# One tile of memory results in place of two, five more row places, and a new table of slots, in a two-branch infini-attention kernel

## The chip, the cores and the metric

The kernel runs on one core of a Trainium2 chip. The metric is the time of one execution on the device in microseconds (us); lower is better. The engines are TensorE (PE; its weight loads are shown apart as PEld), VectorE (DVE), ScalarE (ACT), GpSimd (POOL) and SyncE (SP). All of the transfers that matter here are issued by SP.

## What is computed

Two attention branches A and B read the same input x (2048 tokens, 640 columns) and are mixed by a gate per token. Cut to what matters, the reference is:

```python
def branch(x, wq, wk, wv, wo, beta):             # H = 32 heads of 20, N = 4 segments of L = 512
    q, k, v = heads(x @ wq), heads(x @ wk), heads(x @ wv)
    phi = lambda t: where(t > 0, t + 1, exp(t))
    g, M, z = sigmoid(beta), 0, 0
    for s in range(N):
        p = softmax(q[s] @ k[s].T * 20**-0.5 + causal_mask)
        num, den = phi(q[s]) @ M, phi(q[s]) @ z + 1e-6
        out[s] = g * num / den + (1 - g) * (p @ v[s])
        M, z = M + phi(k[s]).T @ v[s], z + sum(phi(k[s]))
    return merge(out) @ wo
g = sigmoid((x * gate_w).sum(-1))
result = g * branch(x, A...) + (1 - g) * branch(x, B...)
```

## The kernel before

The program is a planner. While it is built, it keeps a clock and a queue for each engine, books every operation with a duration, and writes out the instructions in the order in which its own model would start them. That order is all that is left in the program: each engine runs its list from front to back and waits at semaphores. A duration in the code, such as the 0.9 in `put("D", 0.9, ...)`, is the planner's estimate; it issues nothing and delays nothing by itself.

**Passes, quads and jobs.** The work is eight passes t: segment t // 2 of branch t % 2. Each pass has eight quads of four heads, so 64 quads in all, and quad i is in pass i // 8. For a quad TensorE makes scores twice, first to find row maxima (line 1209, read by DVE in line 1196), then transposed (line 1299, read by ScalarE's exponential in line 1291 and masked by GpSimd in line 1292); then one unit multiplies the probabilities with v (line 1319, 16 calls that are recorded as 32, called the P·V unit here). Between these steps TensorE is filled with projections: a list of jobs in fixed order (`window_jobs`), each a product of one weight tile with five input tiles (line 773 in the helper `product`). For pass t it holds k tile 2, v half 0 (named 0), q and k tiles 3 and 4, v half 1 (named 4), then q and k tiles 0 and 1 of pass t + 1, the five o tiles of pass t - 1, and q tile 2 of pass t + 1. A job that can't start blocks those behind it. Products run in either half of the array, with 64 rows each, so that two run side by side.

**High and low parts.** fp32r products are made exact by splitting: each operand is a rounded high part plus a low part, and a projection adds up 15 terms: five of high by high, five with the weights' low parts, five with the input's low parts.

**Row places.** `big` is a store of NBIG places of one row tile each (128 x 512 fp32, 2 KB a partition). Nearly all that passes through SBUF takes them: input tiles (`want_x`, line 596: three places per tile, one for the load, which goes back, and one each for the high and low part, which stay until 24 jobs of the segment have read them), results of q and k on the way to DRAM, phi(q) and phi(k), attention sums, and the parts for the o projection. The planner loads segment s's input when v half 1 of the last pass of segment s - 1 begins, and asks for it with two places to spare. So at the change of a segment the old input holds 10 places until the last v product has read it, while the new one asks for 15.

**Memory results.** phi(q) times the memory (lines 883 to 900, `mem_unit`, eight units a pass) goes into a tile `O` of 10 KB a partition, five row places' worth. `O_store` has two of them: the next pass's units can write one while the results of this pass wait in the other to be transposed (`o_transpose`, line 925 by way of `turn`) and added to the attention part (line 1496). A tile goes back when its five transposes are made.

**End of a pass.** After a pass's last P·V unit the attention sums, written to DRAM by line 1364, are loaded again (1396, 1398, 1438), weighed by reciprocals (1379, 1384, 1429 or 1430), added to the transposed memory results (1496), split into parts (1420 and 1422 or 1423), and multiplied by o weights. Those weights were mixed in DRAM (571), loaded (552) and split (541, 543).

**The table.** RULES gives for quad i the order of its ten score units, by letters, and seven numbers: the share of the slot over which they are spread, how full DVE's queue may be for late units to start (`calm`), a lag between the two halves, the places that must be free for probabilities (`room`), a shift of the slot (`hold`), and two waits. A quad that is not in it keeps the values of the one ahead of it.

Of the kernel before, what the change touches and what calls it, by code (L numbers as in the profile page):

```python
# [12 lines left out]
F32 = mybir.dt.float32  # L13
# [29 lines left out]
def tile_gated_mix_infini_attn(  # L43
# [156 lines left out]
    def put(e, dur, emit, then=None, prio=5):  # L200
        heapq.heappush(ready[e], (prio, next(seq), dur, emit, then))
        load[e] += dur
        start_next(e)
# [1588 lines left out]
```

## Time and profile before

| what | value |
|---|---|
| three runs | 1014.32, 1015.88, 1016.97 us; median 1015.88 |
| profiled execution | 1016.54 us, of which the profile's span is 1014.8 |
| instructions in the span | 30,827 |
| mean granted TensorE clock | 0.995 |
| data moved by DMA | 241.99 MB, mean 238 GB/s |

The page lists for each engine the time that it was busy in the span, and a chain of waits that ends with the last instruction. A matmul in one half of the array counts TensorE as busy, even when the other half has nothing. In the tables by stretch the columns are the stretch, its length, the busy time of PE, PEld, DVE, ACT and POOL with the number of instructions, the granted clock, the share of DMA time and GB/s. In a timeline a row is start, duration, engine, line, operation, output <- inputs and count, with the idle time ahead of it and what ended that in brackets. Groups by line show the count, busy time in all, and the mean of one in ns.

### The profile page before, as it was taken

To read this page: it belongs to the slowest core of one execution; us is meant where nothing else is said; L and a number is where in the kernel's file an instruction comes from. 1 tells how busy PE (TensorE), PEld (TensorE's weight loads), DVE (VectorE), ACT (ScalarE), POOL (GpSimd) and SP (SyncE) were. 2 spreads that over 40 slices of the span, in tenths; PEclk is the share of its full clock that TensorE was granted. 3 is DMA by queue.
4 is the path that set the end of the run, shared out by engine and by line. 5 is a ranking of instruction groups with operands and counts; after the bars stand their busy time and mean duration, and the time that the engine had idled before them with its cause. 6 is when DMAs were issued, how large, how long until landed. Compare 5 with 4: busy or idle time off the path is not lost.

```text
span 1014.8 us, 30827 instructions
## 1 busy us (share of the span) xinstructions
PE 1002.1 (99%) x11260; PEld 855.5 (84%) x11260; DVE 769.3 (76%) x2604; ACT 659.5 (65%) x1341; POOL 612.3 (60%) x1040
## 2 busy tenths in 40 slices
PE   9999999999999999999999999999999999999998
PEld 7998888888888888878888878897889888878876
DVE  4688777976787778877578976888567897689764
ACT  5376776776566767757766666675676666675672
POOL 4465657676476655775646656486675656567571
PEclk9999999999999999999999999998999999999999
DMA  7999989898896988866768687795876979688531
GB/s 248 308 306 270 298 255 305 274 283 259 262 286 185 286 237 245 268 183 219 237 177 300 188 267 234 206 301 175 252 230 182 313 213 281 206 228 267 151 93 62
DMA packets 148886, 241.99 MB, mean 238 GB/s; under 512 B 13216, under 2 KB 46144, under 8 KB 148416
## 3 DMA queue, kind: packets, MB, share of 16 engines
q1 hardware_dynamic: 148736, 240.03, 77.2%
q8 instruction: 89, 1.46, 0.6%
q14 instruction: 61, 0.50, 0.2%
HBM read 150.83 MB, written 94.65 MB: 242 GB/s over the span
## 4 chain that ended last, share of the span: by engine, by line
PE 84%; DMA 6%; DVE 5%; ACT 1%; POOL 1%; issue 1%; SPq 1%; ACTq 0%; DVEq 0%; POOLq 0%
PE bank L773 50%; PE bank L1319 13%; PE bank L1299 7%; PE bank L1209 7%; PE bank L883 3%; PE bank L965 3%; PE bank L925 2%; DMA row<-dots 1%; DMA dots<-row 1%; DMA kd<-row 1%; DVE bank L1196 1%; PE bank L1234 1%; DVE row L1429 1%; DVE row L1422 1%; DMA row<-in_xT_dram 1%
## 5 line engine op out<-in xcount | busy, mean ns | idle before, releaser
L1196 DVE CUSTOM_DVE_ANT_0 bank<-bank,tri 128x256 f32<-128x256 f32 (+3 forms) x1024 | 474.7, 520 | 150.2 <-PE bank L1209 96.8
L773 PE MATMUL bank<-row,wh 64*128 64x512 f32 x2308 | 498.6, 403 | 0.6 <-DVE mw L897 0.6
L1291 ACT ACTIVATE p<-bank 128x512 f32<-128x512 f32 x588 | 324.0, 601 | 140.0 <-PE bank L1299 108.4
L1292 POOL TENSOR_SCALAR_AFFINE_SELECT p<-p 128x256 f32<-128x256 f32 (+1 forms) x588 | 219.2, 380 | 228.6 <-ACT p L1291 219.2
L773 PEld LDWEIGHTS bank<-row,wh 64*128 64x128 f32 x2308 | 319.8, 186 | 11.8 <-issue 1.1
L773 PE MATMUL bank<-row,wl 64*128 64x512 f32 x1154 | 293.3, 402 | 0.0
L543 POOL TENSOR_TENSOR wl<-wst,wh 128x640 fp32r<-128x640 f32 x115 | 181.3, 1581 | 58.1 <-ACT wh L541 51.7
L1209 PE MATMUL bank<-kst,qst 60*128 60x384 f32 (+3 forms) x1024 | 184.0, 317 | 1.8 <-DVE row L1349 0.8
L773 PEld LDWEIGHTS bank<-row,wl 64*128 64x128 f32 x1154 | 173.6, 186 | 5.0 <-issue 0.6
L1299 PE MATMUL bank<-qst,kst 62*128 62x128 f32 (+3 forms) x1024 | 176.4, 317 | 1.0 <-ACT vst L1015 0.5
L773 PE MATMUL bank<-wvh,row 64*128 64x320 f32 x1280 | 176.7, 312 | 0.0
L1319 PE MATMUL bank<-p,vst 128*32 128x384 f32 (+3 forms) x1936 | 148.9, 431 | 0.0
L773 PEld LDWEIGHTS bank<-wvh,row 64*128 64x128 f32 x1280 | 147.4, 185 | 1.0 <-issue 0.2
L1196 DVE DVE_READ_ACCUMULATOR2_ANT mx<- 128x1 f32 x1024 | 144.6, 141 | 0.0
L1209 PEld LDWEIGHTS bank<-kst,qst 60*128 60x128 f32 x1024 | 137.5, 186 | 8.2 <-DVE row L1349 1.2
L1299 PEld LDWEIGHTS bank<-qst,kst 62*128 62x128 f32 x1024 | 130.5, 186 | 7.3 <-DVE mx L1196 1.0
L1319 PEld LDWEIGHTS bank<-p,vst 128*32 128x32 f32 x1936 | 59.3, 110 | 87.4 <-issue 62.7
L541 ACT CAST wh<-wst 128x640 fp32r<-128x640 f32 x119 | 86.4, 741 | 20.2 <-PE bank L773 14.4
L773 PE MATMUL bank<-wvl,row 64*128 64x320 f32 x640 | 99.3, 310 | 0.0
L1349 ACT COPY row<-bank 128x512 f32<-128x512 f32 x61 | 36.0, 590 | 79.4 <-PE bank L1319 71.1
L773 PEld LDWEIGHTS bank<-wvl,row 64*128 64x128 f32 x640 | 80.0, 185 | 0.6 <-issue 0.4
L518 POOL TENSOR_TENSOR wvl<-wst,wvh 128x640 fp32r<-128x640 f32 (+1 forms) x48 | 64.0, 1338 | 17.3 <-ACT wvh L515 17.3
(117 smaller groups left out, 1213.5 us busy)
## 6 DMA issues: line engine op xcount, KB each, us to landing
qst<-qd SPq DMA_DIRECT2D x128, 240.0 KB
kst<-kd SPq DMA_DIRECT2D x128, 240.0 KB
qd<-row SPq DMA_DIRECT2D x40, 512.0 KB
kd<-row SPq DMA_DIRECT2D x40, 512.0 KB
dots<-row SPq DMA_DIRECT2D x56, 256.0 KB
wst<-wmix SPq DMA_DIRECT2D x35, 320.0 KB
row<-dots SPq DMA_DIRECT2D x42, 256.0 KB
qd<-row SPq DMA_DIRECT2D x40, 256.0 KB
```

Of the source, the lines that this page charges most:

```text
L518: put("G", 0.77 * n, lambda: nc.gpsimd.tensor_tensor(out=wl[:, a:b, :], in0=w3, in1=r32(wh[:, a:b, :]), op=ALU.subtract), end, prio=4)
L541: put("A", 0.625, lambda: nc.scalar.copy(wh, w3), lambda: put(lo_eng, lo_cost, lambda: lo.tensor_tensor(out=wl, in0=w3, in1=r32(wh), op=AL ...
L543: lambda: lo.tensor_tensor(out=wl, in0=w3, in1=r32(wh), op=ALU.subtract), end, prio=3), prio=6)
L773: return nc.tensor.matmul(bank_of, lhsT=w[ROWS[half]], rhs=x_[ROWS[half]], start=start, stop=stop)
L883: return nc.tensor.matmul(pm[:, a - h0:c - h0, :].rearrange("p h e -> p (h e)"), lhsT=r32(pqTs[t, m][ROWS[half], P * n:P * (n + 1)]), rhs= ...
L1196: put("D", w / 960.0 + 0.105, lambda: nc.vector.tensor_tensor_reduce(out=sc[:, off:off + w], in0=sc[:, off:off + w], in1=tri[:, L - w:], s ...
L1209: lane_ops[half].append((mm(w), lambda pair=pair, qb=qb, off=off, w=w, r=r, sc=sc: nc.tensor.matmul(sc[:, off:off + w], lhsT=q[r, pair, P ...
L1291: put("A", 0.483, lambda: nc.scalar.activation(pt, sc, AF.Exp, scale=SCALE), lambda: (bank.give(sc), put("G", 0.15 + 0.105 * len(todo), la ...
L1292: "G", 0.15 + 0.105 * len(todo), lambda: nc.gpsimd.affine_select(out=blocks, in_=blocks, pattern=[[0, len(todo)], [1, P]], base=0, channel ...
L1299: lane_ops[half].append((mm(w), lambda pair=pair, kb=kb, off=off, w=w, r=r, sc=sc: nc.tensor.matmul(sc[:, off:off + w], lhsT=k[r, pair, P ...
L1319: nc.tensor.matmul(po[32 * j:32 * j + 32, P * kb:], lhsT=vst[t % 2][:, kb, h * E1:h * E1 + 32], rhs=pts[i, n, f][0][:, off:off + w], start ...
L1349: either(0.483, lambda: nc.scalar.copy(r32(oT), po), 0.605, lambda: nc.vector.tensor_copy(r32(oT), po), end, 2)
```

## The change

Four things change: `O_store` holds one tile, `NBIG` goes from 29 to 34 (the same memory), six estimates of row operations go up, and every line of the table is new.

```diff
-        4: "TSTSTSTSTS 1.010 1.52 0.31 8 1.9 1.31 1.66",
+        4: "STTSTSSTST 1.010 1.53 0.26 4 0.0 0.35 1",
...
-    NBIG, NWST, NWH, SPARE = 29, 3, 4, 2
+    NBIG, NWST, NWH, SPARE = 34, 3, 4, 2
...
-    O_store = Store([sb.tile([P, NB, D], F32, tag=f"O{i}", name=f"O{i}", bufs=1) for i in range(2)])
+    O_store = Store([sb.tile([P, NB, D], F32, tag=f"O{i}", name=f"O{i}", bufs=1) for i in range(1)])
...
-            put("D", 0.9, lambda: nc.vector.scalar_tensor_tensor(
+            put("D", 1.0, lambda: nc.vector.scalar_tensor_tensor(
                 out=r32(d), in0=r32(d), scalar=gcol[t % 2], in1=r32(g), op0=ALU.mult, op1=ALU.mult), lambda: half(0), prio=2)
...
-                D=(0.85, lambda: nc.vector.tensor_tensor(out=lo, in0=r32(y), in1=r32(hi), op=ALU.subtract)),
-                G=(1.25, lambda: nc.gpsimd.tensor_tensor(out=lo, in0=r32(y), in1=r32(hi), op=ALU.subtract))), prio=2)
+                D=(0.95, lambda: nc.vector.tensor_tensor(out=lo, in0=r32(y), in1=r32(hi), op=ALU.subtract)),
+                G=(1.35, lambda: nc.gpsimd.tensor_tensor(out=lo, in0=r32(y), in1=r32(hi), op=ALU.subtract))), prio=2)
...
-                D=(0.9, lambda: nc.vector.tensor_tensor(out=r32(y), in0=r32(y), in1=r32(r), op=ALU.mult)),
-                G=(1.4, lambda: nc.gpsimd.tensor_tensor(out=r32(y), in0=r32(y), in1=r32(r), op=ALU.mult)))
+                D=(1.05, lambda: nc.vector.tensor_tensor(out=r32(y), in0=r32(y), in1=r32(r), op=ALU.mult)),
+                G=(1.5, lambda: nc.gpsimd.tensor_tensor(out=r32(y), in0=r32(y), in1=r32(r), op=ALU.mult)))
```

The table has one line more in the changed kernel, so line numbers behind it are higher by one there: line 773 of before is line 774.

What this does to the order shows at three places. The first is the change to segment 2 of the input, in pass 3, on two engines. On SP, `dots_119` holds the sums of pass 2, and `dots_120` those of pass 3. Before, the last rows ahead of and with the fifth input load are:

```order
L1364 DMA dots_120<-row_8348_6985 128x512
L1438 DMA row_8370_7010<-dots_119 128x1x512
L1246 DMA qst_82<-mr_163 2x8x128 x2
L552 DMA wst_144<-wmix_130 128x5x128
L1438 DMA row_8448_7075<-dots_119 128x1x512
L1438 DMA row_8466_7090<-dots_119 128x1x512
L1438 DMA row_8487_7106<-dots_119 128x1x512
L1167 DMA qst_81<-qd_100 60x2x512 x2
L596 DMA row_8566_7159<-in_xT_dram 128x512
L1167 DMA kst_85<-kd_108 60x2x512 x2
```

The other four loads stand 13 to 19 rows ahead of that one. In the changed kernel the five stand within nine rows, around the write of the last sums of pass 2:

```order
L597 DMA row_7878_6566<-in_xT_dram 128x512
L1168 DMA qst_83<-qd_100 60x2x512 x2
L1365 DMA dots_119<-row_7966_6631 128x512
L1168 DMA kst_87<-kd_108 60x2x512 x2
L1247 DMA qst_81<-mr_161 2x8x128 x2
L597 DMA row_7883_6569<-in_xT_dram 128x512
L597 DMA row_7946_6611<-in_xT_dram 128x512
L597 DMA row_7963_6630<-in_xT_dram 128x512
L597 DMA row_8006_6666<-in_xT_dram 128x512
L553 DMA wst_142<-in_a_wq_dram 128x640
```

The fifth load has moved from behind the reloads of pass 2's sums to ahead of all of them.

On TensorE at the same change, before, ahead of the first product on the new columns (`row_8112` with `wh`), these rows end a run without any projection; `O` is the tile of memory results, `mbd` the memory, `mt` the row maxima:

```order
L925 MATMUL bank_141<-ident,O_158 128x64 x4
L883 MATMUL bank_135<-mbd_2_77,row_7211_6017 128x21
L883 MATMUL bank_138<-mbd_4_79,row_8327_6960 128x84
L883 MATMUL bank_135<-mbd_3_78,row_7932_6631 128x84
L883 MATMUL bank_135<-mbd_4_79,row_8327_6960 128x84
L1234 MATMUL bank_136<-ident,mt_7269 32x64
L1299 MATMUL bank_139<-qst_82,kst_86 128x512
L1299 MATMUL bank_137<-qst_82,kst_86 128x512
L883 MATMUL bank_135<-mbd_3_78,row_7932_6631 128x84
L1234 MATMUL bank_136<-ident,mt_7269 32x64
L883 MATMUL bank_135<-mbd_4_79,row_8327_6960 128x84
L773 MATMUL bank_141<-row_8112_6774,wh_145 128x512
```

In the changed kernel the products on the new columns (`row_7877` to `row_8004`) alternate with the v products (`wvl`) on the old ones (`row_29..`):

```order
L774 MATMUL bank_135<-row_7944_6609,wl_148 128x512
L1210 MATMUL bank_137<-kst_87,qst_83 128x128
L774 MATMUL bank_138<-wvl,row_2916_2591 128x320
L774 MATMUL bank_135<-row_7961_6628,wl_148 128x512
L774 MATMUL bank_138<-wvl,row_2921_2594 128x320
L774 MATMUL bank_135<-row_8004_6664,wl_148 128x512
L774 MATMUL bank_138<-wvl,row_2926_2597 128x320
L774 MATMUL bank_138<-wvl,row_2931_2600 128x320
L774 MATMUL bank_135<-row_7877_6565,wh_147 128x512
L1300 MATMUL bank_140<-qst_81,kst_85 128x384
```

The run without projections between the two inputs is gone from this place: the q product on the new columns has begun 59 matmuls ahead of the last v product on the old ones, where it stood 82 behind.

The second place is SP's list in pass 1, where the mixed o weights of branch A are made ready for the o jobs of pass 0. Before:

```order
L571 DMA wmix_130<-wrow_128 32x2560
L1364 DMA dots_118<-row_3704_3181 128x512
L571 DMA wmix_130<-wrow_128 32x2560
L1246 DMA qst_83<-mr_163 2x8x128 x2
L752 DMA kd_107<-row_3811_3250 128x2x512
L752 DMA kd_107<-row_3812_3251 128x512
L552 DMA wst_144<-wmix_130 128x5x128
L552 DMA wst_143<-wmix_130 128x5x128
L552 DMA wst_142<-wmix_130 128x5x128
```

And now:

```order
L1168 DMA kst_84<-kd_106 60x2x512 x2
L640 DMA wst_143<-in_x_dram 128x640
L572 DMA wmix_130<-wrow_128 32x2560 x2
L753 DMA kd_107<-row_3583_3110 128x2x512
L753 DMA kd_107<-row_3584_3111 128x512
L553 DMA wst_144<-wmix_130 128x5x128
L553 DMA wst_142<-wmix_130 128x5x128
L553 DMA wst_143<-wmix_130 128x5x128
```

`kd_107` is the DRAM copy of pass 2's k; the write shown is that of its tile 0 in both. The last two mixes now follow each other, a row ahead of that write, and the second write of sums (`dots_118`, of pass 1) no longer stands between them.

The third place is the memory matmuls (line 883) on TensorE. The 44 of a pass stood in two groups, some 50 us of TensorE's work apart; in passes 3 to 7 they now stand together, behind the transposes of the pass before, and in passes 4 and 6 with hardly a projection among them. From pass 4, in the changed kernel:

```order
L774 MATMUL bank_134<-row_8005_6665,wh_145 128x512
L774 MATMUL bank_135<-row_8005_6665,wh_151 128x512
L884 MATMUL bank_141<-mbd_0_70,row_8633_7207 128x84
L884 MATMUL bank_137<-mbd_0_70,row_8633_7207 128x84
L884 MATMUL bank_141<-mbd_1_71,row_8938_7521 128x84
L884 MATMUL bank_137<-mbd_1_71,row_8938_7521 128x84
L884 MATMUL bank_141<-mbd_2_72,row_9624_8093 128x63
```

Eleven more rows of memory matmuls and a P·V unit follow before the rest of them.

119 rows, old and new, of the table RULES are left out of this document.

## The prediction

> **What bounds the kernel now.** I read the page first, then the stretches in which TensorE's projections pause, then the queue that feeds them. The page gives busy time by engine and the chain that ended last.
>
> ```profile
> span 1014.8 us, 30827 instructions
> PE 1002.1 (99%) x11260; PEld 855.5 (84%) x11260; DVE 769.3 (76%) x2604; ACT 659.5 (65%) x1341; POOL 612.3 (60%) x1040
> PE 84%; DMA 6%; DVE 5%; ACT 1%; POOL 1%; issue 1%; SPq 1%; ACTq 0%; DVEq 0%; POOLq 0%
> ```
>
> TensorE is the bound, with 84% of the chain. The 99% hides waits, since a small matmul in one half of the array counts as busy while the other half is empty. So I looked for places where TensorE runs no projection at all. Two stand out, both where segment 2 or 3 of the input begins. In the timeline of TensorE (start, duration, instruction) the last product on the old columns is the v product, line 773 with wvl; the next projection is the first q product on the new ones.
>
> ```profile
> 427.58 0.30 PE L773 MATMUL bank<-wvl,row 64*128 64x320 f32 x1
> 437.87 1.26 PE L773 MATMUL bank<-row,wh 64*128 64x512 f32 x4
> 684.97 0.39 PE L773 MATMUL bank<-wvl,row 64*128 64x320 f32 x1
> 696.20 0.47 PE L773 MATMUL bank<-row,wh 64*128 64x512 f32 x1
> ```
>
> That is 10.3 us and 11.2 us without a projection. What they wait for is the fifth input tile: SP issues its load only once the old columns have been given back, and ScalarE's cast (L586) sits idle until it lands.
>
> ```profile
> 411.00 1.53 SPq L596 DMA_DIRECT2D row<-in_xT_dram  x3
> 428.27 0.40 SPq L596 DMA_DIRECT2D row<-in_xT_dram  x1
> 435.91 0.62 ACT L586 CAST row<-row 128x512 fp32r<-128x512 f32 x1 [2.16 <-DMA row<-in_xT_dram]
> 685.38 1.45 SPq L596 DMA_DIRECT2D row<-in_xT_dram  x1
> 691.55 0.62 ACT L586 CAST row<-row 128x512 fp32r<-128x512 f32 x1 [2.73 <-DMA row<-in_xT_dram]
> ```
>
> Four of five loads are out by 412.5; the fifth leaves at 428.27, within 1 us of the last v product, and lands 7.6 us later. So what is missing is row places, which is what the change adds. The stretches themselves (PE busy, weight loads, DVE, ACT, POOL, granted clock, DMA share, GB/s):
>
> ```profile
> 427.60:437.90 10.30, 8.65 (x122) 6.70 (x119) 10.10 (x28) 6.37 (x14) 8.78 (x10) 1.00 0.91 287
> 437.90:442.00 4.10, 4.10 (x22) 3.22 (x23) 2.77 (x9) 2.17 (x5) 4.10 (x6) 0.58 0.27 73
> 685.00:696.20 11.20, 10.41 (x105) 6.70 (x104) 9.22 (x25) 4.78 (x11) 8.35 (x8) 0.70 0.79 242
> ```
>
> TensorE is truly idle for 1.65 and 0.79 us. The granted clock falls to 0.58 over the 4.1 us behind the first stretch (1.7 us lost) and to 0.70 inside the second (3.4 us lost). The same P·V unit shows it:
>
> ```profile
> 430.74 2.36 PE L1319 MATMUL bank<-p,vst 128*32 128x512 f32 x32
> 691.33 3.86 PE L1319 MATMUL bank<-p,vst 128*32 128x512 f32 x32
> 436.98 0.23 PE L1234 MATMUL bank<-ident,mt 64*32 64x64 f32 x1 [1.59 <-POOL mt L1221]
> ```
>
> **The change, part by part.** The counts of instructions on TensorE are the same before and after; only the order moves.
>
> *Input waits (gain).* The order puts all five loads of segments 2 and 3 ahead of the load of the sums, and the first new product 59 and 48 matmuls ahead of the last v product, where it stood 82 and 69 behind. Does the data come in time?
>
> ```profile
> 400.58 1.16 PE L1319 MATMUL bank<-p,vst 128*32 128x384 f32 x20
> 426.50 0.40 PE L773 MATMUL bank<-row,wh 64*128 64x512 f32 x1
> 426.74 0.40 PE L773 MATMUL bank<-row,wh 64*128 64x512 f32 x1
> 402.91 0.58 SPq L1364 DMA_DIRECT2D dots<-row  x1
> 417.77 0.62 ACT L586 CAST row<-row 128x512 fp32r<-128x512 f32 x1 [0.68 <-DMA qst<-qd]
> L590 POOL TENSOR_TENSOR row<-row,row 128x512 fp32r<-128x512 f32 x15 | 19.6, 1320 | 2.2 <-ACT row L586 2.2
> ```
>
> Between the P·V unit of quad 23 and that product the order now has 43 products of 512 columns, 100 of 320, 36 scores, 20 transposes and one P·V unit. A 512-column product of one half takes 0.24 us, from the two starts, so 0.12 us with both halves in use, and the shorter ones (scores have 320 on the mean) in proportion; with the P·V unit, 2.3, that is 18 us. "Us of work" is counted in this way from here on.
>
> The write of quad 23's sums goes out 1.2 us after its P·V unit ended (401.7); two small writes and four loads later it is about 5 us. From the last of the three loads (412.1) to the last cast's end was 6.3 us, so high parts by about 12 us and, at 1.3 us each on GpSimd (L590), low parts by 17, which the product needs only at its eleventh term. It fits, with some 3 us to spare; quad 39 has 17 us and fits likewise.
>
> What is saved? The work inside the stretches is not removed but goes beside projections: in the first, one P·V unit, 42 transposes, 19 memory matmuls (two passes each) and 4 scores; in the second one P·V unit, 36, 14 and 2.
>
> ```profile
> 433.72 0.47 PE L925 MATMUL bank<-ident,O 64*128 64x64 f32 x8
> 434.74 0.65 PE L883 MATMUL bank<-mbd,row 64*128 64x84 f32 x6
> ```
>
> Eight transposes take 0.47 us of which 0.22 is one's own length, so 0.036 apart; memory passes (0.65 - 0.27)/5 = 0.076. First stretch: 2.3 + 42 x 0.036 + 38 x 0.076 + 4 x 0.12 = 7.2 of 10.3 us, saved 3.1. Second: 2.3 + 1.3 + 2.1 + 0.2 = 5.9 of 11.2, saved 5.3 with its own half-rate clock in it. With 1.7 for the clock behind the first: **10.0 us**. The lower bound is idle time and clock alone, 2.4 + 5.1 = 7.5. The upper: beside projections the small matmuls take one of two halves and cost half, which saves 5.5 + 7.1 + 1.7 = 14.3. I take the middle, as the rows just read are the nearest.
>
> Rows for the clock's part stand above: 1.59 us of idle, and the lower clock follows directly. [...]
>
> *One tile of memory results (cost).* The memory matmuls of a pass now wait until the pass before has handed back the tile. In passes 4 and 6 all 44 stand within 6 us of work, in 3, 5 and 7 within 19; before they were split over some 50. Each of eight units needs three operations on DVE:
>
> ```profile
> L897 DVE SCALAR_TENSOR_TENSOR mw<-bank,gq 128x19 f32<-128x19 f32 (+1 forms) x48 | 8.1, 168 | 9.4 <-PE bank L883 9.4
> L899 DVE RECIPROCAL mw<-mw 128x19 f32<-128x19 f32 (+1 forms) x48 | 12.4, 258 | 1.6
> L900 DVE TENSOR_TENSOR O<-bank,mw 128x380 f32<-128x380 f32 (+1 forms) x48 | 23.6, 491 | 1.6
> ```
>
> That is 0.92 us, 7.3 for eight, and the banks stay taken meanwhile. Their cover is the q and k jobs of the next pass. In passes 4 and 6 DVE needs 1.3 us more than TensorE has work; I take **1.0 us** in all, with 0 (the next products cover it) and 12.5 (the second rival) as ends.
>
> *The o jobs of pass 0 (cost).* They now begin 37 us of work after that pass's last P·V unit, before 49. Their weights come by a chain that the trace shows whole:
>
> ```profile
> 188.60 0.86 SPq L571 DMA_DIRECT2D wmix<-wrow  x1
> 194.87 1.84 SPq L552 DMA_DIRECT2D wst<-wmix  x3
> 202.06 1.36 ACT L541 CAST wh<-wst 128x640 fp32r<-128x640 f32 x2
> 202.87 3.08 POOL L543 TENSOR_TENSOR wl<-wst,wh 128x640 fp32r<-128x640 f32 x2 [0.23 <-ACT wh L541]
> L965 PE MATMUL bank<-vst,row 64*128 64x147 f32 (+1 forms) x480 | 64.3, 293 | 0.0
> L733 ACT ACTIVATE row<-row 128x512 f32<-128x512 f32 x25 | 16.1, 656 | 0.1
> ```
>
> From the last mix to the first low part (202.87 + 1.54) it is 15.8 us. In the new order that mix stands just ahead of the write of k tile 0, whose product ends 14 us of work before the first o product (60 products, 18 scores, 26 transposes, one P·V unit, and 22 updates of two passes at half of 64.3/480 us); with 2 us for taking that product out of its bank the mix may go 12 to 16 us ahead. So TensorE waits 0 to 4 us; I take **0.5**, as SP has few rows there to be held by.
>
> *The rest.* The planner's raised costs (0.9 to 1.0 and so on) issue nothing; they and the table act by the order alone. Nine more phi tiles take the way with a second activation (L733): 9 x 0.656 = 5.9 us more on ScalarE, hidden since it is 65% busy, and 5.9 if it bound. Behind the last P·V unit 8.4 us of work stand, before 9.65; the end is a chain of transposes and DVE, so I count nothing (0 to +1).
>
> The sum: -10.0 + 1.0 + 0.5 = -8.5 us. The profiled execution took 1016.54 (span 1014.8 and 1.7 around it), 0.66 above the median of 1015.88, so 1008.0 for it and **1007.4** against the median.
>
> **Rivals.** One more row, of the low part that ended pass 2's chain:
>
> ```profile
> 441.11 1.29 POOL L1423 TENSOR_TENSOR row<-row,row 128x512 fp32r<-128x512 f32 x1
> ```
>
> - *The wait moves on to the o jobs* (1013.5). The o products of pass 2 come 42 us of work after quad 23's P·V unit, before 47; in the trace the last low part came 40.7 us after it (442.4). For: four input loads and two weights now stand ahead of the sums. Against: the five loads of rows are no longer held for places. Three us late at passes 2 and 4, and the weights' ends above, give back 6.
> - *The bunched memory units hold TensorE* (slower, 1020). At five boundaries DVE takes 7.3 us of memory units in one go, and the row maxima (L1196) queue behind; in the first stretch DVE was busy for 10.10 of 10.30 us. If TensorE stands for 2.5 us at each, 12.5 us are added. It makes the change a loss from 2 us at each on. Against: the planner starts no such unit while DVE's queue is long.
> - *The small matmuls cost half* (1002): the upper bound of the gain with both costs at nothing.
> - That places still lack is excluded by the order, unless the loads themselves come late.
>
> **How the numbers follow.** A measurement here tells about 0.3%, 3 us, from no change: faster is below 1012.8, slower above 1018.9. Forecast 0.60 (by itself 1002 to 1012), the wait that moves 0.20, bunching 0.13, half cost 0.07. All of the forecast and the half cost, and 0.08 of the moved wait, are faster: 0.75. The rest of the moved wait, 0.12, is the same; bunching, 0.13, slower. The range 1000 to 1017 leaves out bunching and about 0.05 below.
>
> **What would show it.** The five input loads of segments 2 and 3 stand together on SP, none after the last v product; no stretch of 10 us without line 773 at these places; a granted clock of 1.00 at both; PE's share of the chain up, DMA's down. Wrong: a new stretch without projections before the first o product of pass 0, 2 or 4, or DVE near 100% with TensorE waiting on line 897 or 1196 after the transposes of O.

## The result, and the profile after

The changed kernel takes **1017.18 us** (median of 18 runs, 1014.32 to 1019.94), the kernel before 1014.27 in the same comparison (18 runs, 1012.20 to 1016.97). The ratio is 1.0026, with a 95% interval of 1.0017 to 1.0035: 2.9 us slower, where 1007.4 had been forecast.

Nearly every sign that the prediction named for its main step came true all the same. The page of the changed kernel, busy times and chain:

```profile
span 1016.0 us, 30827 instructions
...
PE 1004.5 (99%) x11260; PEld 859.7 (85%) x11260; DVE 766.3 (75%) x2593; ACT 663.9 (65%) x1352; POOL 612.5 (60%) x1040
...
PE 89%; DMA 4%; DVE 4%; ACT 1%; issue 1%; SPq 0%; POOL 0%; DVEq 0%; POOLq 0%; ACTq 0%
```

TensorE's share of the chain rose from 84 to 89%, DMA's fell from 6 to 4%, and the mean granted clock is 0.999. On SP the loads of segments 2 and 3 stand together:

```profile
405.79 1.86 SPq L597 DMA_DIRECT2D row<-in_xT_dram  x4
...
660.87 3.40 SPq L597 DMA_DIRECT2D row<-in_xT_dram  x5
```

The stretches around the two segment changes (the same columns as in the prediction) show TensorE idle for 0.39 us of the first 22, for none of the others, and a granted clock of 1.00:

```profile
413.00:435.00 22.00, 21.61 (x245) 18.94 (x242) 16.38 (x45) 14.47 (x30) 15.53 (x21) 1.00 0.95 291
...
670.00:692.00 22.00, 22.00 (x242) 19.93 (x240) 19.80 (x48) 16.25 (x34) 17.72 (x21) 1.00 0.88 288
692.00:711.00 19.00, 19.00 (x242) 16.98 (x238) 17.38 (x49) 12.89 (x26) 11.68 (x18) 1.00 0.93 309
```

So what the prediction took for a wait is gone, and the kernel is slower. To see where the time went I counted TensorE's work at the prediction's prices (0.12 us for a product of 512 columns and in proportion for shorter ones and scores, 2.3 for a P·V unit, 0.036 for a transpose, 0.076 for a memory pass, 0.067 for an update pass; 977.4 us in both kernels) and took it from the time between P·V units. What is left over is loss: waits, an empty half, a low clock. Here it is by pass, each from the end of the last P·V unit of the pass before to the end of its own:

| loss in us, profiled execution | pass 0 | 1 | 2 | 3 | 4 | 5 | 6 | 7 | behind | sum |
|---|---|---|---|---|---|---|---|---|---|---|
| before | 7.6 | 2.0 | 1.9 | **6.5** | 1.9 | **5.3** | 0.3 | 6.4 | 5.6 | 37.4 |
| changed | 7.6 | 4.4 | 3.3 | 3.4 | 1.8 | 1.6 | 2.9 | 7.4 | 6.2 | 38.6 |

The passes with a change of input (3 and 5) lose 6.8 us less, about what TensorE's idle time and the low clock took in that execution of before (7.5 by the prediction), and not 10. Passes 1, 2, 6 and 7 lose 7.4 us more. The prices are estimates. If the small matmuls are counted by their columns alone, passes 3 and 5 gain 5.9 us, pass 1 loses 1.5 and pass 6 again 2.6, but pass 2 then gains 1.6 and pass 7 loses 3.7, so of these two the table says little. (By these two executions the changed kernel is 1.2 us behind, by the medians 2.9: the one of before took 1016.54, 2.3 above its median.)

One more view decides how this is to be read. Each execution comes with its mean granted clock. Over the 90 executions of before in all comparisons with the experiments the mean is 0.9966 (0.993 to 0.998); the one that the prediction was made from had 0.995. Over 18 executions of the changed kernel it is 0.9995. The difference, 0.0029 of 1014, is 2.9 us of clock gained, if TensorE is what counts throughout. So, by this estimate, everything else got worse by 2.9 + 2.9 = 5.8 us. (Among the executions with six added matmuls, below, 0.0063 of clock goes with 4.2 us of time; by that rate it would be 1.9 and 4.8.)

### The profile page after: what moved, and what is told of

The parts are those of the page before. It is cut to its first block, busy times and chain, and to the rows that moved or that the text cites. A ratio compares the mean times of both kernels' runs of the same rounds, so it can differ in the third digit from the quotient of the medians.

```text
span 1016.0 us, 30827 instructions
## 1 busy us (share of the span) xinstructions
PE 1004.5 (99%) x11260; PEld 859.7 (85%) x11260; DVE 766.3 (75%) x2593; ACT 663.9 (65%) x1352; POOL 612.5 (60%) x1040
## 4 chain that ended last, share of the span: by engine, by line
PE 89%; DMA 4%; DVE 4%; ACT 1%; issue 1%; SPq 0%; POOL 0%; DVEq 0%; POOLq 0%; ACTq 0%
PE bank L774 52%; PE bank L1320 14%; PE bank L1300 7%; PE bank L1210 7%; PE bank L966 3%; PE bank L884 3%; PE bank L926 2%; DMA kd<-row 1%; DVE bank L1197 1%; PE bank L1235 1%; DMA row<-dots 1%; DMA qd<-row 1%; DVE row L1430 1%; DMA row<-rowg 1%; DMA wst<-in_a_wk_dram 1%
## 5 line engine op out<-in xcount | busy, mean ns | idle before, releaser
L1197 DVE CUSTOM_DVE_ANT_0 bank<-bank,tri 128x384 f32<-128x384 f32 (+3 forms) x1024 | 473.9, 520 | 155.2 <-PE bank L1210 121.5
L774 PE MATMUL bank<-row,wh 64*128 64x512 f32 x2308 | 507.2, 403 | 1.2 <-DVE mx L1197 0.7
L1292 ACT ACTIVATE p<-bank 128x512 f32<-128x512 f32 x568 | 312.4, 599 | 138.4 <-PE bank L1300 108.4
L774 PEld LDWEIGHTS bank<-row,wh 64*128 64x128 f32 x2308 | 323.8, 185 | 12.5 <-issue 1.3
L774 PE MATMUL bank<-row,wl 64*128 64x512 f32 x1154 | 298.0, 399 | 0.0
L774 PE MATMUL bank<-wvh,row 64*128 64x320 f32 x1280 | 181.3, 312 | 0.0
L1300 PE MATMUL bank<-qst,kst 62*128 62x512 f32 (+3 forms) x1024 | 178.2, 318 | 1.9 <-DVE mw L898 0.7
L1320 PE MATMUL bank<-p,vst 128*32 128x512 f32 (+3 forms) x1896 | 142.1, 424 | 0.0
L1210 PEld LDWEIGHTS bank<-kst,qst 60*128 60x128 f32 x1024 | 132.4, 186 | 8.9 <-DVE mx L1197 4.0
L774 PE MATMUL bank<-wvl,row 64*128 64x320 f32 x640 | 104.5, 310 | 0.0
```

The costliest lines, as they stand in the source:

```text
L774: return nc.tensor.matmul(bank_of, lhsT=w[ROWS[half]], rhs=x_[ROWS[half]], start=start, stop=stop)
L1197: put("D", w / 960.0 + 0.105, lambda: nc.vector.tensor_tensor_reduce(out=sc[:, off:off + w], in0=sc[:, off:off + w], in1=tri[:, L - w:], s ...
L1210: lane_ops[half].append((mm(w), lambda pair=pair, qb=qb, off=off, w=w, r=r, sc=sc: nc.tensor.matmul(sc[:, off:off + w], lhsT=q[r, pair, P ...
L1292: put("A", 0.483, lambda: nc.scalar.activation(pt, sc, AF.Exp, scale=SCALE), lambda: (bank.give(sc), put("G", 0.15 + 0.105 * len(todo), la ...
L1300: lane_ops[half].append((mm(w), lambda pair=pair, kb=kb, off=off, w=w, r=r, sc=sc: nc.tensor.matmul(sc[:, off:off + w], lhsT=k[r, pair, P ...
L1320: nc.tensor.matmul(po[32 * j:32 * j + 32, P * kb:], lhsT=vst[t % 2][:, kb, h * E1:h * E1 + 32], rhs=pts[i, n, f][0][:, off:off + w], start ...
```

## The experiments

Three theories stood against each other at first. A: the places save what was forecast and the new table gives it away. B: one tile of memory results costs about what the places bring. C: a table fits only the order that it was found with. In all that follow "before" is the kernel before, run on the same chip in the same rounds.

### What the table does

The first two exchange the tables between the kernels; the last two give both the same single line for all slots:

```diff
     RULES = {
-        0: "STTSTSSTST 1.010 1.71 0.30 8 0.0 1.73 1",
...
+        0: "TSTSTSTSTS 1.010 2.38 0.30 8 0.0 1.6 1",
     }
```

> The changed kernel with the table of slots of before; one tile of memory results, 34 places and the raised estimates stay. Theory A (the places save what was forecast, some 7 to 9 us, and the new table gives it away by shifting small waits): 1006 to 1010. Theory B (one tile of memory results costs about as much as the five places bring, whatever the table): 1014 to 1020. Theory C (each table fits only the order that it was found with, and any other loses some us): 1018 to 1026, above the changed kernel's 1017.2.

> The kernel before with the new table only. Theory A (the new table gives away what the places bring): 1020 to 1024, since the 7 to 9 us that the table costs are then without the places' gain. Theory B (the table does nothing by itself): 1012 to 1017. Theory C (a table fits only its own order): 1018 to 1026.

> The kernel before with one line for all 64 slots, the values that most lines of both tables have, so that no slot is set by hand. Only the difference from the next run counts for the stores; its height over 1014.3 is what the table of before is worth: A and B 1014 to 1020, C 1020 or more.

> The changed kernel with the same single line for all slots. Against the run before it, Theory A (places save, the new table loses): 7 to 9 us faster. Theory B (one tile costs what the places bring): within 3 us, or slower. Theory C says nothing of the sign, but both stand some 5 us or more above 1014.3.

| kernel | median, us | ratio to before (95%) | planner's own end, us |
|---|---|---|---|
| before | 1015.25 | 1 | 1005.4 |
| changed | 1017.18 | 1.0026 (1.0017 to 1.0035) | 1005.9 |
| changed, table of before | 1064.58 | 1.0479 (1.0456 to 1.0501) | 1048.5 |
| before, new table | 1068.87 | 1.0521 (1.0494 to 1.0548) | 1050.5 |
| before, one line | 1059.68 | 1.0431 (1.0407 to 1.0456) | 1043.5 |
| changed, one line | 1059.22 | 1.0451 (1.0416 to 1.0485) | 1048.6 |

The planner's own end is the clock that the program keeps while it is built; it is no measured time. All four missed what A and B expected, and the exchanged tables cost much more than C had allowed: each table is worth some 45 us to the stores and estimates that it was found with. The wrong table is 9 us worse than one line in before, and in the changed kernel no better than one line. With one line for all slots the stores make no difference that shows: 1059.68 and 1059.22 us, uncertain by some 4. Two things follow. A change of four parts can't be taken apart by undoing one, since each part alone makes a new plan without its table. And the planner had reckoned with the missing places all along, since it books them itself: by its own clock the two plans end 0.5 us apart.

So the remaining experiments leave the order alone. They change what an instruction does, not when the planner books it, and each engine's list stays the same but for what the edit names.

### Is the stretch a wait?

The fifth input tile of segments 2 and 3 is not loaded; its cast reads a tile that is there:

```diff
-                put("A", 0.515, lambda: nc.scalar.copy(hi, r32(st)), low, prio=6)
+                put("A", 0.515, lambda: nc.scalar.copy(hi, r32(src)), low, prio=6)
...
-            dma(0.87, lambda: nc.sync.dma_start(
+            dma(0.87, lambda: None if skip else nc.sync.dma_start(
```

> The kernel before with its order of instructions unchanged, but the fifth input tile of segments 2 and 3 is left out: its two loads are not issued, and its casts read the first tile's high part, which is there. So the result is computed from a wrong fifth tile; what is measured is the time without the transfer's 7.6 us. Theory W (the two stretches cost the 2.4 us of idle and the 5.1 of lower clock, and their other work costs the same wherever it stands): 1007 to 1010. Theory F (the forecast's fuller gain, 10 or more): 1004 or less. Theory N (the wait is made up for behind it): 1013 or more.

> The same omission in the changed kernel, whose fifth loads stand with the other four: a control. If the five more places have taken the input waits away, nothing is left to gain: 1016 to 1018. If the loads still hold TensorE there, 1010 to 1014. As in the run before it, the fifth tile of segments 2 and 3 is wrong.

Before without the fifth loads: 1014.61 us, ratio 1.0000 (0.9988 to 1.0012). The changed kernel: 1016.51, ratio 1.0020 (1.0010 to 1.0031). Theory N was right for before: **the transfer of the fifth tile costs nothing there.** The timeline of before without it shows why. The cast no longer waits, but TensorE still runs 8.6 us of other work between its last v product and the next q product:

```profile
426.83 0.30 PE L778 MATMUL bank<-wvl,row 64*128 64x320 f32 x1
435.46 0.97 PE L778 MATMUL bank<-row,wh 64*128 64x512 f32 x4
...
432.90 0.62 ACT L591 CAST row<-row 128x512 fp32r<-128x512 f32 x1
```

Its stretches (the columns as before) show the first one full at a clock of 1.00, and the second as before, with the clock at 0.70 on the mean, though there is nothing to load:

```profile
426.80:435.50 8.70, 8.62 (x123) 6.76 (x119) 8.64 (x22) 6.54 (x14) 8.70 (x11) 1.00 0.92 288
...
682.10:693.60 11.50, 10.43 (x106) 6.75 (x106) 9.33 (x25) 4.82 (x11) 8.35 (x8) 0.70 0.68 214
```

And the idle time of the first stretch differs between executions. Here it is in the seventh run (e7), which keeps the order and the fifth load of before and leaves out some work of DVE: the load lands 6.0 us after its issue instead of 7.6, ScalarE waits 0.45 us for it instead of 2.16, and the stretch (its row stands behind the two of the timeline) is full at a clock of 1.00:

```profile
426.51 0.40 SPq L596 DMA_DIRECT2D row<-in_xT_dram  x1
...
432.47 0.62 ACT L586 CAST row<-row 128x512 fp32r<-128x512 f32 x1 [0.45 <-DMA row<-in_xT_dram]
```

```profile
425.90:434.50 8.60, 8.52 (x120) 6.66 (x117) 8.57 (x22) 6.34 (x14) 8.60 (x10) 1.00 0.88 289
```

From P·V unit 24 to 26 the profiled execution of before took 40.4 us; with the same instructions there, two other profiled executions took 37.2 (e10, where TensorE idles for 0.08 us in the stretch) and 38.5 (e9, 0.81 us, with the clock at half for 3.4 us behind it). So the wait is real in some executions and absent in others.

### Do the bunched memory units hold TensorE?

Two of a memory unit's three operations on DVE are left out:

```diff
-            nc.vector.scalar_tensor_tensor(
-                out=w, in0=pm[:, :nh, DH], scalar=1e-6, in1=gq[t][:, n, h0:h1], op0=ALU.add, op1=ALU.mult)
-            nc.vector.reciprocal(w, w)
+            w = gq[t][:, n, h0:h1]
```

> The kernel before, order unchanged, without two of the three DVE operations of each memory unit (the weights with the normaliser, 168 ns, and their reciprocal, 258 ns): the memory result is multiplied by the gates alone, so it is not normalised. 96 operations and about 20 us of DVE fewer. Theory B (memory units in one go on DVE hold TensorE): within 2 us of 1014.3, since they are spread here. If DVE's lateness at every boundary counts, whatever the units' spread: 1009 to 1012.

> The same omission in the changed kernel, where the eight units of a pass stand together. Theory B (bunched units hold TensorE, 2 to 3.5 us at some of five boundaries): 3 to 6 us faster than the changed kernel, 1011 to 1014, and clearly more than the run before it gains. Theory R (what the change loses is many small shifts of the order, not these units): the same gain as in the run before it, 0 to 2 us.

Before: 1013.31 us, ratio 0.9984 (0.9973 to 0.9996). Changed: 1016.25, ratio 1.0019 (1.0008 to 1.0030). The first gains 0.16%, 1.6 us; the second, from 1.0026, 0.07%, 0.7 us. If the bunched units held TensorE, the changed kernel would gain more, not less. Theory B is out, and with it the mechanism of the prediction's slower rival. The pair also shows that some 20 us less work on DVE does not by itself bring the two kernels together.

### What is the clock worth, and what lets it fall?

Six and twelve matmuls were added where TensorE stands in the second stretch, all into unused columns of a memory unit's bank:

```diff
+    FILL = {('mem', 161): 1, ('mem', 164): 1, ('S', 703): 1, ('mem', 167): 3}
...
+        for _ in range(FILL.get((kind, seen[kind]), 0)):
+            nc.tensor.matmul(last[:, 400:], lhsT=ident, rhs=ident[:, :112], start=True, stop=True, skip_group_check=True)
```

> The kernel before with six more matmuls (128 rows, 112 columns, into unused columns of the memory unit's bank) in the second stretch, where TensorE stands for 0.3 and 0.35 to 0.65 us and the granted clock then falls to 0.50 for 3.3 to 6.8 us. Theory K (what the change gained is the lower clock of this stretch, and TensorE's standing there lets it fall): the clock stays up, the mean clock of the runs goes from 0.9967 to 0.999, and the time from 1014.6 to 1011.5 to 1012.5. If the small matmuls themselves pull the clock down: the six cost up to 1 us and the clock is as before, 1014.5 to 1015.5.

> The same with twelve. Theory K: the clock stays up, but the twelve need some 2 us and the standing covers 1: 1012.5 to 1013.5. Otherwise 1015 to 1016.5.

With six, 1015.82 us, ratio 1.0009 (0.9994 to 1.0024); with twelve, 1014.90, ratio 1.0001 (0.9984 to 1.0018). The medians say nothing; the clocks do. No execution of before, of 90, had a mean clock above 0.998. With six added matmuls 6 of 12 had 1.000 (mean span 1011.9 us), and 4 had 0.993 or 0.994 (1016.1). With twelve, 9 of 11 had 1.000. The stretch in the profiled execution of each, six first, then twelve:

```profile
682.00:694.00 12.00, 11.83 (x89) 9.38 (x89) 10.61 (x35) 6.07 (x12) 8.86 (x10) 0.70 0.89 283
```

```profile
682.00:694.00 12.00, 11.88 (x140) 9.15 (x139) 10.39 (x29) 5.68 (x12) 8.91 (x10) 1.00 0.83 250
```

So twelve added matmuls keep the clock up in nine executions of eleven, and six in half of them. That TensorE's standing is what lets it fall, as the prediction took it, is not shown. In the execution with six, TensorE stood for 0.17 us in these 12 us, and the clock was at half for 10.2 us. In before the clock fell at 687.6, ahead of the second standing. And without DVE's multiplications (e11, below) TensorE stood for 0.81 us at the same place, and the clock stayed up:

```profile
683.00:691.00 8.00, 7.19 (x105) 5.00 (x104) 6.77 (x21) 4.61 (x11) 7.14 (x8) 1.00 0.92 290
```

The twelve matmuls (two records each) took 3.7 us themselves, in the timeline of their own execution:

```profile
684.01 0.70 PE L871 MATMUL bank<-ident 128*128 128x112 f32 x4
685.37 0.70 PE L871 MATMUL bank<-ident 128*128 128x112 f32 x4
686.82 0.92 PE L871 MATMUL bank<-ident 128*128 128x112 f32 x6
688.10 1.37 PE L871 MATMUL bank<-ident 128*128 128x112 f32 x10
```

That is about what they saved: from P·V unit 40 to 42 it is 42.2 us with and without them (45.5 in the execution with six). Theory K was right that the clock can be held up there and wrong on the profit; what lets it fall stays open.

The clock was at half for 6.8 us in before (687.6 to 694.4), for 3.4 in e7 (685.2 to 688.6) and for 10.2 in e9 (686.8 to 697.0). In e7 TensorE had stood for 0.32 and 0.65 us ahead of that. What sets these lengths was not shown either.

### DVE's row operations

TensorE's first standing in that stretch (0.31 us) was for DVE, the second (0.35 us) for ScalarE. In before a multiplication of two rows took 1.92 us while GpSimd worked on a weights' low part, and the addition behind it, which gives back the bank, came late:

```profile
684.98 1.54 POOL L543 TENSOR_TENSOR wl<-wst,wh 128x640 fp32r<-128x640 f32 x1 [0.17 <-ACT wh L541]
...
685.14 1.92 DVE L1429 TENSOR_TENSOR row<-row,row 128x512 f32<-128x512 f32 x1
686.99 0.68 DVE L1496 TENSOR_TENSOR row<-bank,row 128x512 f32<-128x512 f32 x1
...
687.72 0.80 PE L1209 MATMUL bank<-kst,qst 60*128 60x512 f32 x2 [0.31 <-DVE row L1496]
```

Is that common? The groups of such operations show it, here the low parts of before; the line of 0.69 us is the same kind of operation early in the kernel:

```profile
L1422 DVE TENSOR_TENSOR row<-row,row 128x512 fp32r<-128x512 f32 x16 | 18.2, 1148 | 0.0
...
L590 DVE TENSOR_TENSOR row<-row,row 128x512 fp32r<-128x512 f32 x5 | 3.4, 692 | 2.0 <-ACT row L586 1.9
```

Sorted by whether GpSimd ran a two-operand operation during more than a tenth of them, the 40 operations of before take 0.74 us on the mean (10, none beside) and 1.24 (30, up to 1.92), those of the changed kernel 0.76 (10) and 1.31 (30, up to 1.93). It is not only operations of two operands: the one-operand copies of the runs below take 0.42 us alone, and 1.01 (e13) and 1.07 (e14) on the mean beside GpSimd's. The traces show that the long ones go with GpSimd's work, not how it slows them. In all, the 40 operations take 44.7 us in before and 46.9 in the changed kernel.

Theory D: these operations, with the row maxima queued behind them, are what the changed order loses by. Two pairs of runs leave them out, first the multiplications alone, then all that stand at the end of a pass:

```diff
-                D=(0.9, lambda: nc.vector.tensor_tensor(out=r32(y), in0=r32(y), in1=r32(r), op=ALU.mult)),
+                D=(0.9, lambda: None),
```

```diff
-            put("D", 0.9, lambda: nc.vector.scalar_tensor_tensor(
-                out=r32(d), in0=r32(d), scalar=gcol[t % 2], in1=r32(g), op0=ALU.mult, op1=ALU.mult), lambda: half(0), prio=2)
+            put("D", 0.9, lambda: None, lambda: half(0), prio=2)
...
-                D=(0.85, lambda: nc.vector.tensor_tensor(out=lo, in0=r32(y), in1=r32(hi), op=ALU.subtract)),
+                D=(0.85, lambda: nc.vector.tensor_copy(lo, r32(hi))),
```

> The kernel before, order unchanged, without the 12 multiplications by reciprocals that stand on DVE (line 1429; 0.96 to 1.92 us each, the long ones while GpSimd works on rows too), so these rows of the attention part stay unweighed. Theory D (DVE's row operations at the end of a pass hold the row maxima, and so TensorE): 1.5 to 3 us faster, mostly in the second stretch, whose first standing is behind the one of 1.92 us. If they are hidden: within 1 us of 1014.6.

> The same omission in the changed kernel, which has 14 of them on DVE. Theory D (what the changed order loses at quads 9, 40, 49 and 58 stands behind these operations): 3 to 5 us faster than 1017.2, more than the run before it gains. If the loss has other causes: at most as much as the run before it gains.

> The kernel before, order unchanged, without DVE's row operations of two operands in SBUF at the end of a pass: the 12 multiplications by reciprocals and the 7 gatings are left out, and the 16 low parts are copies of the high part (one operand). 41 us of DVE less some 10 for the copies. Theory D (these hold row maxima and so TensorE): 1007 to 1010, little below the run that left out the multiplications alone (1009.9), since before has its stall behind one of those. Theory O (the order itself): no less than that run.

> The same omission in the changed kernel (14 multiplications, 7 gatings, 14 low parts on DVE). Theory D: the difference between the two kernels goes away, 1007 to 1010, and the steps at quads 49 and 58, which stand behind a gating of 1.93 and a low part of 1.80 us, are gone. Theory O: the changed kernel stays 2 to 3 us above the run before it, 1010.5 to 1013, and the steps stay.

| left out on DVE | before, us | ratio to before (95%) | changed, us | ratio to before (95%) |
|---|---|---|---|---|
| nothing | 1014.27 | 1 | 1017.18 | 1.0026 (1.0017 to 1.0035) |
| multiplications | 1009.87 | 0.9954 (0.9939 to 0.9970) | 1012.89 | 0.9983 (0.9968 to 0.9997) |
| all three kinds | 1011.31 | 0.9960 (0.9943 to 0.9976) | 1010.12 | 0.9948 (0.9934 to 0.9963) |

The multiplications alone (0.69 to 1.92 us each in before, where the expectation says 0.96 to 1.92) gain 0.46% in before (4.7 us) and 0.43% in the changed kernel (4.4), more than was expected of before and no more in the changed one: on this pair Theory D failed. In before they also end the second stretch's stall: 39.1 us from P·V unit 40 to 42 instead of 42.2, with the clock at 1.00 where it had been at half for 6.8 us. With gatings and low parts gone too, the changed kernel gains 0.78% (7.9 us) and before 0.40% (4.1; 1011.3 where Theory D had expected 1010 at most), and the changed one is no longer the slower: by the two ratios it stands at 0.9988 of the other, uncertain by 0.0022. **The difference of +0.26% has become -0.12%**, a shift of 0.38% with 0.24% of uncertainty (the three half widths of the intervals, 0.09, 0.165 and 0.145, as the root of their squares): 3.9 us of the 5.8, uncertain by 2.4. By the middle value Theory O is out for the larger part of the loss. The copies that replace the low parts still take 14.9 and 13.6 us, so what was left out is 26 us of DVE in before and 30 in the changed kernel.

The waits for DVE's row maxima (`mx`) say more than the times. A score can't take its bank before the row maximum of an earlier one has been read out of it. These are the weight loads of scores that stood for that (us in all, how often, the longest), before first, then changed, then changed without the row operations (e14):

```profile
PEld bank L1299 <- DVE mx L1196: 1.0, 3, 0.5
PEld bank L1209 <- DVE mx L1196: 0.4, 2, 0.2
```

```profile
PEld bank L1210 <- DVE mx L1197: 4.0, 9, 0.9
PEld bank L1300 <- DVE mx L1197: 2.5, 6, 0.8
```

```profile
PEld bank L1210 <- DVE mx L1197: 0.5, 2, 0.3
PEld bank L1300 <- DVE mx L1197: 0.2, 1, 0.2
```

The sums are alike in all profiled executions of the two orders: 1.4 to 2.0 us in the seven of the order of before that keep some or all of these operations, 4.2 to 6.5 in the five such of the changed order, and 0.2 and 0.7 with all three kinds left out. Without the multiplications alone it is still 4.3 in the changed order (e12), which fits that pair's result. Weight loads waited while earlier matmuls still ran: in the changed kernel the matmuls of these two lines stood for 1.2 and 0.7 us where their weight loads stood for 4.0 and 2.5, so not all of this is TensorE's time.

A place that shows it is behind P·V unit 48, in pass 6. In the changed kernel a gating takes 1.93 us beside GpSimd's low part, the row maximum queued behind it comes late, and the two scores that need its bank wait:

```profile
796.25 1.56 POOL L544 TENSOR_TENSOR wl<-wst,wh 128x640 fp32r<-128x640 f32 x1
...
796.43 1.93 DVE L1380 SCALAR_TENSOR_TENSOR row<-row,gcol,row 128x512 f32<-128x512 f32 x1 [0.96 <-DMA row<-dots]
798.28 0.69 DVE L1197 CUSTOM_DVE_ANT_0 bank<-bank,tri 128x512 f32<-128x512 f32 x1
...
798.10 0.33 PE L1210 MATMUL bank<-kst,qst 60*128 60x384 f32 x1
799.08 0.44 PE L1210 MATMUL bank<-kst,qst 60*128 60x384 f32 x2 [0.65 <-DVE mx L1197]
```

Without the row operations (e14) the same scores follow the same fifteen v products at once:

```profile
791.63 1.33 PE L774 MATMUL bank<-wvh,row 64*128 64x320 f32 x15
792.77 0.42 PE L1210 MATMUL bank<-kst,qst 60*128 60x384 f32 x4
```

Times between P·V units of the changed order, which can be compared directly since the lists are the same: from 48 to 49 it is 24.2, 23.1 and 23.0 us in the changed kernel, e6 and e8, and 22.2 in e14; from 39 to 40 it is 16.0, 15.5 and 16.4, and 15.2; from 57 to 58 it is 16.7, 16.7 and 16.8, and 16.4. The gating of 1.93 us took 0.78 in e6 and 0.79 in e8, so of the 2.0 us between 24.2 and 22.2 half belongs to one execution. By the count of loss by pass, the changed order loses 2.6 us more than that of before in pass 6, and 0.5 more without the row operations (e14 against e13). In pass 1 it is 2.4 and 3.3: that loss has another cause, which stays open.

The last two runs move the multiplications instead of leaving them out, a candidate for a version better than both:

```diff
-                D=(0.9, lambda: nc.vector.tensor_tensor(out=r32(y), in0=r32(y), in1=r32(r), op=ALU.mult)),
+                D=(0.9, lambda: nc.gpsimd.tensor_tensor(out=r32(y), in0=r32(y), in1=r32(r), op=ALU.mult)),
```

> The kernel before with the 12 multiplications issued to GpSimd at the same place of the order, all of the result computed. Theory D: DVE's row maxima come earlier, 1010 to 1013, if GpSimd (60% busy) can take 12 x 1.3 us where they stand. If GpSimd's masks and low parts are then late: 1016 to 1022.

> The same in the changed kernel, 14 multiplications. Theory D: 1013 to 1016. If GpSimd is late: 1018 to 1024.

1020.81 us, ratio 1.0057 (1.0040 to 1.0074), and 1018.82, ratio 1.0038 (1.0023 to 1.0054). So GpSimd can't take them at these places for nothing; how they lose was not taken apart. In the first the gatings on DVE grew from 1.05 to 1.21 us on the mean, and the mean clock fell to 0.9937, which by the two rates above is 2 to 3 of the 5.8 us. No kernel with the whole result beat the kernel before.

## Why the prediction was wrong, point by point

- **Input waits, -10.0 us: the right sign, too large.** The step that was mis-sized is "What is saved?". I read a stretch without projections as a wait. The loads, the order and the clock went as forecast, but the stretch was full of other work, and that costs about the same elsewhere: passes 3 and 5 together lose 6.8 us less, no more than the lower bound of 7.5, "idle time and clock alone", and the 2.5 us above it did not come. That bound was itself too high for most executions, because it rested on one. It had a mean clock of 0.995 where the mean of 90 is 0.9966, and 2 to 3 us in the first stretch that other executions of the same instructions don't have (40.4 against 37.2 and 38.5). Over many executions the clock alone is worth 2.9 us; what is left of the idle time was not measured by itself. The fifth transfer, taken away with the order unchanged, is worth 0 (1.0000, 0.9988 to 1.0012).
- **What ends the second stretch's wait.** The prediction said the fifth load in both. In the second it was not: without the load the clock still fell to 0.70, and without DVE's multiplications, one of them 1.92 us long there, the clock stayed at 1.00 and the stretch took 3.1 us less.
- **One tile of memory results, +1.0 us: not contradicted, not measured by itself.** The bunched units came as the order showed, and lightening them gains no more in the changed kernel (0.7 us) than in before (1.6). Nor does TensorE wait among those that the changed kernel runs together in pass 4, ahead of pass 5's q tile 1:

```profile
562.51 1.96 PE L884 MATMUL bank<-mbd,row 64*128 64x84 f32 x32
564.40 2.36 PE L1320 MATMUL bank<-p,vst 128*32 128x512 f32 x32
...
567.98 2.01 PE L884 MATMUL bank<-mbd,row 64*128 64x84 f32 x28
```

  1.96 / 32 and 2.01 / 28 are 0.061 and 0.072 us a pass, about the 0.076 that the prediction had read, and not half of it. The rival of the half cost, with its gain of 14.3 us, did not come; what such matmuls cost beside projections, which it spoke of, was not measured.
- **The o jobs of pass 0, +0.5 us: right, by one execution.** The stretch ahead of the first o product, in the changed kernel:

```profile
193.86 1.42 PE L774 MATMUL bank<-row,wh 64*128 64x512 f32 x10
201.23 0.49 PE L774 MATMUL bank<-row,wh 64*128 64x512 f32 x1
```

  The last of the ten started at about 194.9; of the 6.3 us from there to the first o product 5.7 are counted work, so 0.6 are lost.
- **"The rest", 0 us: wrong, about +4.3 or more. This is the step that turned the sign.** It is the 5.8 us less the 1.5 forecast for the two terms above, if those hold; what the input waits saved beyond the clock comes on top. The prediction said that the raised costs (five estimates, not six) and the table "act by the order alone", which is true, and then priced the order at three places of 64 quads and put the others at nothing without a reason. The order is what counts: a table that doesn't fit costs 45 us. About 3.9 us of the loss, uncertain by 2.4, are DVE's row operations: with them the scores of the new order wait 4.2 to 6.5 us for row maxima, where those of the old one wait 1.4 to 2.0, and without them 0.7 and 0.2.
- **The rivals.** The wait that moves on to the o jobs did not come: in passes 3, 5 and 7 of the changed kernel, where the o products of passes 2, 4 and 6 stand, the longest stretch without projections is 3.9 us, and of those over 2.3 us none has more than 0.8 that is no counted work. The slower rival had the right sign and the wrong mechanism; DVE's queue does hold scores, but by row operations of up to 1.93 us and not by memory units.

What stays open: some 2 us of the 5.8 (5.8 less 3.9, which is uncertain by 2.4), the loss in pass 1, and why more scores of the new order stand close behind these operations, which are hardly longer there (46.9 us in all against 44.7). Both kernels also have 14 reciprocals of 1.74 us in DVE's queue, which no run left out. What one tile and 34 places are worth with a table found for the old estimates was not tried.

## What to carry to other kernels

A stretch in which the main work pauses is a wait only as far as the engine stands idle or slow in it; if a planner or a hand has filled it, closing it moves the filling. Price the idle time, and from several executions: one profile held 2 to 3 us here that others of the same instructions didn't have. Where an order is tuned as a whole, a change of one resource is worth the difference between two tuned orders, and that is to be asked of the whole program, not of the place where the resource was short.

## What was not expected of the hardware

- The granted clock fell to half amid small matmuls and transposes, where TensorE had stood for no longer than 0.65 us at a time (e7), and stayed there for 3.4, 6.8 or 10.2 us. With 0.17 us of standing it fell (e9), with 0.81 it did not (e11). The mean clocks say that it falls in every execution of before (0.993 to 0.998), and little or not in the changed kernel (0.999 or 1.000 in all 18). With six matmuls of 112 columns added, 6 of 12 executions had a mean of 1.000.
- The two-operand row operations in SBUF took 0.74 and 0.76 us on the mean on DVE alone, and 1.24 and 1.31, up to 1.93, beside GpSimd's. Some are long again and again: the multiplication of before takes 1.92 us in its own profile, 1.92 in e5 and 1.93 in e7. Others are not: the gating of 1.93 us in the changed kernel takes 0.78 in e6 and 0.79 in e8.
- Executions of one kernel differ by 5 us (1012.1 to 1017.4 in 35 of before), and the 2 to 3 us of the first stretch are part of that.
